# Row sums in a PSUM tile of their own, the first gathers moved ahead of a check, and fewer filler matmuls, in an attention and mixture-of-experts kernel

## The chip, the cores and the metric

The kernel runs on one core of one Trainium2 chip. The metric is the device time of one execution in microseconds (us), the median over several runs. Where the text gives a clock, it is the granted clock of TensorE: the share of full speed that the chip gave it, as a mean over the run or over the stretch named.

## The reference, cut to what matters

```python
# attention: 4 batches, 8 heads, 768 positions, head size 64; 8 global keys and a band of 96
scores = q @ k.T / 8 + bias;  a = softmax(scores where kept);  o = a @ v
x = o laid out as 3072 tokens x 512
# experts: 8, each takes exactly 384 tokens, chosen greedily by the sorted gate logits
logits = x @ w_gate
for (token, e) in sorted(logits, descending):
    if token is free and counts[e] < 384: assign it
out[tokens of e] = relu(x[tokens of e] @ w1[e]) @ w2[e]     # 512 -> 1024 -> 512
```

## The kernel before

Attention works on 16 pairs of heads. For the first six pairs the token rows are made at once: TensorE sums the weights of each row (`sums`), turns the output to token rows (`pn`), VectorE turns the sums (`dg`), takes the reciprocal (`rs`) and writes the scaled rows (`xb`). Sums and rows share one tile in PSUM, the buffer into which all these matmuls write. There are three such tiles in a ring (tag "ps"), and the scores of the next pair go through the same ring.

```python
        def token_matmuls(i, ot):
            ...
            pn = ps.tile([128, 8, 128], FP32, tag="ps", name=f"pn{i}")
            NS = S_ // 4
            sums = pn[:, 6:8, :].rearrange("p a x -> p (a x)")[:, 0:NS]
            ...                                   # 12 matmuls into sums
            if i < N_ATTN:
                token_transposes(pn, ot)          # 6 transposes into pn[:, 0:6]
            return pn, sums

        def gate_terms(i, sums):
            ...
            nc.vector.transpose(out=dg.rearrange("p c x -> p (c x)"), in_=sums)
            nc.vector.reciprocal(rs, dg[:, :, 0:2])
            ...
        def token_rows(i, pn, rs):                # xb = pn * rs
```

After the routing, the index of each expert's tokens is written (`idi`), then a flag that says whether the fast routing was valid (`fi`). GpSimd gathers the tokens by index, 128 rows at a time, three gathers for each expert. While the first ones are on the way, TensorE runs filler matmuls, meant to keep its clock up (with 2 of them, in fill2, the mean clock was 0.968 or 0.969 in all four runs; with 12, in fill12, 0.981 to 0.984 in all five).

```python
        nc.vector.tensor_single_scalar(out=idi, in_=pI, scalar=float(N_TOK // 2), op=ALU.add)
        if check is not None:
            ...
            nc.vector.tensor_single_scalar(out=fi, in_=fm, scalar=capf, op=ALU.is_gt)
    ...
        dispatch(tX, tR, tZ[:, 1, :])
        keep_busy(po[0], 14)
    ...
    gather(0)
    flag = nc.values_load(fi[0:1, 0:1], engines=mybir.ALL_ENGINES)
    ...
        with tc.manual_schedule(engines={ET.PE, ET.DVE, ET.Activation}):
            gather(1)
            to_columns(0)      # per gather: 4 transposes (px), copy to xT, then keep_busy(spare, 2)
            for e in range(N_EXP):
                layer1(e)                          # 32 matmuls into ph, ScalarE writes hT
                for _ in range(2):
                    next_weights(nc.vector)        # cast staged weights, start the next load
                if e + 2 < N_EXP:
                    gather(e + 2)
                if e + 1 < N_EXP:
                    to_columns(e + 1)              # 12 transposes (pxe)
                layer2(e)
                next_weights(nc.scalar)
```

The softmax here doesn't subtract the row's maximum and nothing guards it: scores larger than these inputs give would overflow.

## Time and profile before

| | before |
|---|---|
| time, median (range) | 283.92 us (283.36 to 284.98) |
| span of the profiled run | 284.8 us; that run itself took 286.62 us |
| TensorE busy | 261.7 us, 92% |

The profiled run is 2.7 us longer than the median of the timed ones. It has a stop of TensorE in the second expert.

The hand-over to the experts in the timeline of the kernel before. The columns are start (us), duration, engine, line, operation, written tile and read tiles, shapes, count, and in brackets the idle time before and what ended it. PE is TensorE, PEld its weight loads, DVE VectorE, ACT ScalarE, POOL GpSimd; "issue" means that nothing was seen to be waited for:

```profile
178.95 0.18 DVE L315 TENSOR_SCALAR idi<-bank 128x24 int32<-128x24 f32 x1 [0.38 <-PE bank L314]
179.60 0.14 DVE L319 TENSOR_SCALAR fi<-fm 1x1 int32<-1x1 f32 x1
180.02 1.26 POOL L873 DMA_INDIRECT xe<-x_tok,idi  x1 [42.03 <-DVE fi L319]
...
186.79 1.47 POOL L873 DMA_INDIRECT xe<-x_tok,idi  x1 [0.30 <-issue]
186.93 2.36 DVE L508 CAST w<-st 128x2048 bf16<-128x2048 f32 x2
```

The indices are there at 179.13 (178.95 + 0.18). The first gather starts 0.89 us later and is said to wait for fi. The line at 186.79 is the sixth gather, the last one for the second expert. The line under it is VectorE's two casts of weights.

### The profile page before, as it was taken

Reading aid. Unit: us, or ns where it says so; the run is one execution under the profiler, and the core shown is the slowest. Engines: PE = TensorE matmul, PEld = TensorE weight load, DVE = VectorE, ACT = ScalarE, POOL = GpSimd, SP = SyncE. Lnnn points to the kernel's source line nnn. Section 1 sums busy time; section 2 is a strip of 40 time slices with the busy share of each in tenths; the row PEclk is TensorE's granted clock in tenths of the full one; section 3 lists DMA queues with packets and bytes.
Section 4 is the critical chain, followed back from the end, with each engine's and each line's share of the span. In section 5 each row is a group of like instructions: output and inputs, shape, how many; then the busy total and the mean of one; then the engine's idle time right before and its main releaser. Section 6 shows DMA issues by size and latency. Waiting matters only on the chain. (4 is left out here: it accounts for less than half of the span.)

```text
span 284.8 us, 7265 instructions
## 1 busy us (share of the span) xinstructions
PE 261.7 (92%) x2890; PEld 178.2 (63%) x2890; DVE 182.5 (64%) x349; ACT 155.4 (55%) x256; POOL 128.9 (45%) x170
## 2 busy tenths in 40 slices
PE   7899999999999999999988885999699999999990
PEld 5777777777788787778756552355355556556550
DVE  3466978887788778887988889143444535635420
ACT  1888665575777777776125665043347347356330
POOL 8469425552455555533100000577675663513512
PEclk9999999999999999999999999599999999999998
DMA  7989997696759678220298777259899999996112
GB/s 175 267 193 224 261 274 213 170 319 214 210 146 247 200 241 244 77 77 3 87 396 296 204 275 254 64 184 378 265 349 400 387 387 377 383 333 270 74 59 88
DMA packets 58340, 65.98 MB, mean 232 GB/s; under 512 B 32960, under 2 KB 43712, under 8 KB 58304
## 3 DMA queue, kind: packets, MB, share of 16 engines
q1 hardware_dynamic: 53664, 55.67, 63.3%
q0 software_dynamic: 3072, 9.44, 8.6%
q10 hardware_dynamic: 1568, 0.39, 0.7%
q8 instruction: 23, 0.38, 0.6%
q14 instruction: 13, 0.11, 0.1%
HBM read 56.05 MB, written 9.44 MB: 230 GB/s over the span
## 5 line engine op out<-in xcount | busy, mean ns | idle before, releaser
L930 ACT ACTIVATE hT<-ph 128x384 bf16<-128x384 f32 x64 | 30.9, 490 | 52.1 <-PE ph L927 50.7
L873 POOL DMA_INDIRECT xe<-x_tok,idi x24 | 25.4, 1060 | 54.9 <-DVE fi L319 42.0
L619 ACT ACTIVATE P<-ps 128x860 f32<-128x860 f32 (+1 forms) x48 | 41.3, 892 | 14.4 <-PE ps L612 13.3
L612 PE MATMUL ps<-qT,kT 64*128 64x215 f32 (+2 forms) x448 | 44.1, 337 | 2.8 <-DVE qT L601 1.1
L927 PE MATMUL ph<-xT,w 128*128 128x384 bf16 x256 | 43.7, 326 | 3.1 <-issue 2.4
L945 POOL DMA_INDIRECT out_dram<-ot,idi x24 | 30.6, 1275 | 31.0 <-DVE ot L944 27.4
L942 PE MATMUL po<-w,hT 128*128 128x512 bf16 (+1 forms) x200 | 42.8, 370 | 0.0
L612 PEld LDWEIGHTS ps<-qT,kT 64*128 64x128 f32 x448 | 36.6, 187 | 8.8 <-PE ps L612 2.6
L627 DVE TENSOR_TENSOR P<-P,Wm 128x860 f32<-128x860 f32 (+1 forms) x32 | 32.6, 1055 | 11.7 <-ACT P L619 11.4
L669 PE MATMUL po<-P,vt 128*32 128x215 f32 (+4 forms) x1024 | 38.8, 302 | 0.0
L927 PEld LDWEIGHTS <-w 128*128 128x128 bf16 x256 | 25.0, 98 | 21.2 <-issue 4.3
L593 POOL COPY kT<-kT 128x56 f32<-128x56 f32 x16 | 11.6, 724 | 56.7 <-ACT kT L590 41.3
L669 PEld LDWEIGHTS po<-P,vt 128*32 128x32 f32 x1024 | 29.7, 110 | 9.7 <-issue 2.5
L944 DVE COPY ot<-po 128x512 f32<-128x512 f32 (+1 forms) x25 | 16.7, 670 | 28.5 <-PE po L942 20.2
L508 ACT CAST w<-st 128x1024 bf16<-128x1024 f32 (+1 forms) x23 | 33.4, 1451 | 0.0
L942 PEld LDWEIGHTS <-hT 128*128 128x128 bf16 x200 | 19.3, 98 | 20.4
L918 DVE COPY xT<-pxe 128x1536 bf16<-128x1536 bf16 x7 | 6.7, 958 | 22.4 <-PE pxe L917 22.4
L601 ACT COPY qT<-ptq 128x768 f32<-128x768 f32 x15 | 12.0, 802 | 16.2 <-PE ptq L580 16.2
L638 DVE TENSOR_TENSOR R<-P 128x950 f32<-128x950 f32 x16 | 18.9, 1180 | 0.0
L624 DVE TENSOR_TENSOR P<-P,Wm 128x860 f32<-128x860 f32 x16 | 16.9, 1055 | 2.0 <-DVE P L627 0.5
L508 DVE CAST w<-st 128x2048 bf16<-128x2048 f32 x15 | 18.0, 1239 | 0.0
L169 PE MATMUL po<-busy,c_ones_bf 128*128 128x512 bf16 x58 | 17.9, 433 | 0.0
(166 smaller groups left out, 362.9 us busy)
## 6 DMA issues: line engine op xcount, KB each, us to landing
st<-in_moe_w_dram SPq DMA_DIRECT2D x26, 1024.0 KB
st<-in_moe_w_dram SPq DMA_DIRECT2D x12, 512.0 KB
kr<-in_k_dram SPq DMA_DIRECT2D x15, 384.0 KB
qr<-in_q_dram SPq DMA_DIRECT2D x15, 384.0 KB
vt<-in_v_dram SPq DMA_DIRECT2D x32, 180.0 KB
x_tok<-xb SPq DMA_DIRECT2D x4, 768.0 KB
vt<-in_v_dram SPq DMA_DIRECT2D x32, 14.0 KB
qn<-in_q_dram ACTq DMA_DIRECT2D x2, 192.0 KB
```

The source lines that it names most:

```text
L169: nc.tensor.matmul(tile, lhsT=cs.ones_bf, rhs=cs.busy, start=True, stop=True)
L508: put(out=wt[n][:, a * half : a * half + a, :].rearrange("p a f -> p (a f)"), in_=st)
L612: nc.tensor.matmul(pt[:, t, off : off + widths[m]], lhsT=kk[64 * t : 64 * t + 64, m, :], rhs=qq[64 * t : 64 * t + 64, KT * m : KT * m + wi ...
L619: nc.scalar.activation(P, pt[:, :, 0:off], AF.Exp, scale=0.125)
L627: nc.vector.tensor_tensor(out=P, in0=P, in1=Wm[:, h0 : h0 + 2, w0 : w0 + off], op=ALU.mult)
L638: nc.vector.tensor_tensor(out=R[:, :, KT : 6 * KT].rearrange("p t (m q) -> p t m q", q=KT)[:, :, :, 0:tail], in0=P[:, :, QW : 6 * QW].rear ...
L669: nc.tensor.matmul(po[bank][64 * t + 32 * u : 64 * t + 32 * u + 32, c0 : c0 + n], lhsT=vv[:, t, m, 32 * u : 32 * u + 32], rhs=P[:, t, pc : ...
L873: nc.gpsimd.indirect_dma_start(out=xe_of[e][t], out_offset=None, in_=x_tok[:, :], in_offset=bass.IndirectOffsetOnAxis(ap=idi[:, TSLAB * e ...
L927: nc.tensor.matmul(ph, lhsT=w1_of(e)[:, kc, 128 * fc : 128 * fc + 128], rhs=xT_e[:, kc, :, :].rearrange("p t n -> p (t n)"), start=(kc == ...
L930: nc.scalar.activation(hT[:, fc, :], ph, AF.Relu)
L942: nc.tensor.matmul(po[:, 0:w], lhsT=hT[:, fc, 128 * t : 128 * t + 128], rhs=w2_of(e)[:, fc, c0 : c0 + w], start=(fc == 0), stop=(fc == NFC ...
L945: s = nc.gpsimd.indirect_dma_start(out=out[:, :], out_offset=bass.IndirectOffsetOnAxis(ap=idi[:, TSLAB * e + t : TSLAB * e + t + 1], axis= ...
```

## The change

The change has three parts. The row sums get a PSUM tile apart from the token rows (part A). The first expert's gathers go into the hand-made order, ahead of the count check (part B). The fillers go from 14 to 10, and from 2 to 1 between the transposes of the first expert (part C).

```diff
         nc.vector.tensor_single_scalar(out=idi, in_=pI, scalar=float(N_TOK // 2), op=ALU.add)
         if check is not None:
+            gather(0)
             nc.vector.tensor_reduce(out=fc8, ...)
 ...
-            pn = ps.tile([128, 8, 128], FP32, tag="ps", name=f"pn{i}")
+            pd = ps.tile([128, 2, 512], FP32, tag="ps", name=f"pd{i}")
             NS = S_ // 4
-            sums = pn[:, 6:8, :].rearrange("p a x -> p (a x)")[:, 0:NS]
+            sums = pd[:, 0, 0:NS]
 ...
-            if i < N_ATTN:
-                token_transposes(pn, ot)
-            return pn, sums
+            return sums
 ...
-                    pn, sums = token_matmuls(i - 2, oT[i - 2])
+                    sums = token_matmuls(i - 2, oT[i - 2])
                     rs = gate_terms(i - 2, sums)
                     if i - 2 < N_ATTN:
+                        pn = ps.tile([128, 8, 128], FP32, tag="ps", name=f"pn{i - 2}")
+                        token_transposes(pn, oT[i - 2])
                         token_rows(i - 2, pn, rs)
 ...
-        keep_busy(po[0], 14)
+        keep_busy(po[0], 10)
 ...                              # the definition of gather moves up, its call gather(0) goes from here
-    gather(0)
     flag = nc.values_load(fi[0:1, 0:1], engines=mybir.ALL_ENGINES)
 ...
-                        keep_busy(spare, 2)
+                        keep_busy(spare, 1)
```

More of the change, by code (lines that the diff above doesn't have):

```diff
@@ L817 @@
             add_tiles(NP - 1)
-            pn, sums = token_matmuls(NP - 2, oT[NP - 2])
+            sums = token_matmuls(NP - 2, oT[NP - 2])
             later.append((NP - 2, oT[NP - 2], gate_terms(NP - 2, sums)))
@@ L821 @@
             ot = attend(NP - 1)
-            pn, sums = token_matmuls(NP - 1, ot)
+            sums = token_matmuls(NP - 1, ot)
             later.append((NP - 1, ot, gate_terms(NP - 1, sums)))
@@ L846, in next_weights, with gather @@
                 fetched.append(fetch(stage, *late.pop(0)))
+    gp = ctx.enter_context(tc.tile_pool(name="gp", bufs=9))
+    xe_of = {}
+    def gather(e):
+        if e not in xe_of:
+            xe_of[e] = [gp.tile([128, DM], BF16, tag="xe", name=f"xe_{TSLAB * e + t}") for t in range(TSLAB)]
+        for t in range(TSLAB):
+            nc.gpsimd.indirect_dma_start(
+                out=xe_of[e][t], out_offset=None, in_=x_tok[:, :],
+                in_offset=bass.IndirectOffsetOnAxis(ap=idi[:, TSLAB * e + t : TSLAB * e + t + 1], axis=0),
+                bounds_check=N_TOK - 1, oob_is_err=False,
+            )
     with tc.manual_schedule(engines={ET.PE, ET.DVE, ET.Activation, ET.Pool}):
@@ L859 @@
         dispatch(tX, tR, tZ[:, 1, :])
-        keep_busy(po[0], 14)
+        keep_busy(po[0], 10)
     psx.close()
     kx.close()
-    gp = ctx.enter_context(tc.tile_pool(name="gp", bufs=9))
-    xe_of = {}
-    def gather(e):
-        if e not in xe_of:
-            xe_of[e] = [gp.tile([128, DM], BF16, tag="xe", name=f"xe_{TSLAB * e + t}") for t in range(TSLAB)]
-        for t in range(TSLAB):
-            nc.gpsimd.indirect_dma_start(
-                out=xe_of[e][t], out_offset=None, in_=x_tok[:, :],
-                in_offset=bass.IndirectOffsetOnAxis(ap=idi[:, TSLAB * e + t : TSLAB * e + t + 1], axis=0),
-                bounds_check=N_TOK - 1, oob_is_err=False,
-            )
-    gather(0)
     flag = nc.values_load(fi[0:1, 0:1], engines=mybir.ALL_ENGINES)
```

## The prediction

> **What bounds the kernel now.** I read the page's slices and its chain first, then the timeline stage by stage. The chain reaches back only to 184.66 us: it is the tail of the expert stage, where TensorE hardly stops. Before that lie attention (0 to 138 us), five routing rounds with the dispatch (138 to 179) and the hand-over to the first expert (179 to 187). So whatever is saved before 187 us should move the end by as much, if the stages in between keep their length. I looked for TensorE's stops in the two stages that the diff touches.
>
> Attention: the list of waits between 10 and 138 us (engine, line, what it waited for, total us, times, longest):
>
> ```profile
> DVE dg L709 <- PE pn L701: 7.9, 6, 1.7
> DVE dg L709 <- PE pn L691: 4.7, 7, 0.8
> PE ps L612 <- DVE xb L735: 0.8, 4, 0.3
> ```
>
> Six times VectorE's transpose of the row sums (dg) waits for the token transposes (L701), though it reads only what L691 wrote. TensorE in turn waits for the scaled copy xb before it may reuse the tile. TensorE's timeline (start, us, line, count), first a pair with token rows, then one without:
>
> ```profile
> 45.75 0.87 PE L701 MATMUL pn<-ident,oT 128*128 128x128 f32 x6
> 46.56 1.87 PE L612 MATMUL ps<-qT,kT 64*128 64x215 f32 x20
> 48.62 1.18 PE L612 MATMUL ps<-qT,kT 64*128 64x215 f32 x8 [0.19 <-DVE xb L735]
> ...
> 81.80 2.60 PE L612 MATMUL ps<-qT,kT 64*128 64x215 f32 x28
> 84.32 0.88 PE L580 MATMUL ptk<-ident,kn 128*128 128x128 f32 x6
> ```
>
> and VectorE beside the first of these:
>
> ```profile
> 46.66 0.38 DVE L709 STREAM_TRANSPOSE dg<-pn 128x192 f32<-128x192 f32 x1 [1.31 <-PE pn L701]
> ...
> 47.52 0.95 DVE L735 TENSOR_TENSOR xb<-pn,rs 128x768 bf16<-128x768 f32 x1
> ```
>
> The printed 0.19 us understates the stop. By starts, the 28 score matmuls take 2.52 us without token rows (81.80 to 84.32); with them 3.07, 2.98, 3.17, 2.99, 3.41 and 2.99 us in the six pairs.
>
> Hand-over:
>
> ```profile
> 178.73 5.83 PE L169 MATMUL po<-busy,c_ones_bf 128*128 128x512 bf16 x14
> 184.86 0.38 PE L907 MATMUL px<-c_ident_bf,xe 128*128 128x128 bf16 x4 [0.30 <-PEq L881]
> ...
> 186.16 0.39 PE L907 MATMUL px<-c_ident_bf,xe 128*128 128x128 bf16 x4
> 187.06 1.14 PE L927 MATMUL ph<-xT,w 128*128 128x384 bf16 x6 [0.51 <-issue]
> ```
>
> Fourteen filler matmuls fill the time until the gathered rows arrive; each takes 0.427 us, twice the 0.215 us between the fillers at 185.08. The windows' granted clock says why: 1.00 until 177.25, 0.50 until 184.0, then 1.00.
>
> [...]
>
> **The change part by part.**
>
> A, a tile of its own for the row sums (six pairs). No instruction is added or removed. In the built programs dg waits for the 12 row-sum matmuls instead of the 6 transposes behind them, and the transposes' wait is taken up by xb. At 46 us: the row sums end at 45.82 (45.31 + 0.51), so dg starts at about 45.86, not 46.66; VectorE had been idle since 45.36. xb keeps its 0.86 us behind dg: 46.72, just after the transposes' end at 46.62. It ends at 47.67, not 48.47. The next 8 score matmuls want to start at 48.15: 46.56 plus 1.59, which is 2.52 less the 0.93 us that 8 such matmuls take where nothing waits (30.89 to 31.82). Before, 48.62 was xb's end plus 0.15; now that would be 47.82, so the stop of 0.47 us goes. Over the pairs: 0.55, 0.46, 0.47, 0.47 and 0.47 us, **2.4 us**. The fifth pair (3.41) stops on an issue gap before xb matters, and 0.18 us of the third lies behind the wait; I leave both. The price is one more turn of three buffers. The pn tile now waits for ScalarE's copy of ptk, done some 3 us before (51.55 against 54.80 in the next pair); the scores behind it wait for the qT copy (45.60 against 46.5); the next wait for dg (46.24). None should bind. The later pairs, 7.59 us each, are TensorE back to back, so they only start earlier.
>
> B, the first gathers ahead of the count check. The page puts the gather's start at 180.02 on fi, which ends 0.61 us after idi, so the move seems worth 0.6 us. But the built programs are alike here: in both, GpSimd's gather waits for vector count 286, which idi raises; fi is 289. GpSimd's own order is the same too. **0 us.** The profile named the vector instruction that ended last before it.
>
> C, fewer fillers: 14 to 10, and 2 to 1 twice. Four fewer at 0.427 are 1.7 us: TensorE reaches the first transposes at about 183.15 instead of 184.86. There the data take over: the windows show the third gather's bytes between 184.5 and 185.5, so its transposes can't start before about 185.45, against 186.16. The first layer then starts near 186.35, not 187.06: **0.7 us**.
>
> Sum: 2.4 + 0 + 0.7 = 3.1 us off 283.9.
>
> **The rivals.** (1) The clock stays at half. Fillers now run 4.2 us instead of 5.9[...]. In the trace, the window from 177.3 to 180.7 had fillers for 57% of its length and did not bring the clock back[...]. If it fails, the first layer runs at half speed for some 3.4 to 6.8 us after 186.35, and costs half of that, 1.7 to 3.4 us, nearly all of the gain. I give this one chance in four for a given run. (2) A new wait in the buffer ring: the scores at 46.5 depend on VectorE (dg) where they depended on ScalarE. VectorE has 1.3 us of idle time ahead of each dg, which speaks against it; it would leave A near 1 us. (3) The saving is taken back later: the loads of the next pairs, or the weights. TensorE waits once for a load in attention (0.2 us), and no cast of weights waits in the expert stage; since all stages shift together I see no room for it. TensorE does stop for 1.9 us at 200.4 in the second expert, for a reason the trace doesn't name; if that follows the transfers and not TensorE, up to 0.7 us of C is lost. (4) B is real after all, and all three gathers start 0.6 us earlier: then C is worth 1.3 and the time is 280.2.
>
> **Range and chances.** 283.9 - 3.1 = 280.8; rival 1 at one in four with some 2.5 us adds 0.6, the issue gaps and (4) take away a little. I say **281.0 us**. Low end 279.6: A 3.1, C 1.3. High end 283.2: A halved, or the clock late in most runs. Two per cent faster is 278.2, 5.7 us less, more than all parts together at their best (A 3.5, B and C 1.3): chance 0.04. Slower by 2% needs a new wait in every pair: 0.02. Within 2%: 0.94.
>
> **What would show it.** A: dg starts right behind L691, its waits for L701 are gone, L612 no longer waits for xb, and the pair period falls from about 8.9 to 8.4 us; attention's end moves from 138 to about 135.6. B: the first gather still starts about 0.9 us after idi's end. C: the third px starts about 6.3 us after idi's end (7.0 before) and the clock is back to 1.00 before the first L927. I am wrong if L612 or L701 waits for DVE or ACT in the six pairs, if L927's first 32 matmuls take well over 5.5 us, or if the saving made by 138 us is no longer there at 180.

## The result, and the profile after

| | before | changed |
|---|---|---|
| time, median (range) of the same rounds | 283.84 us (283.36 to 284.98) | 280.99 us (280.20 to 281.95) |
| ratio of fast runs, 95% interval | | 0.9895 (0.9853 to 0.9938) |
| span of the profiled run | 284.8 us | 278.4 us (the fastest of its four runs) |

A ratio is the mean time of one kernel's fast runs over that of the other's in the same rounds, so it is not quite the ratio of the medians. The gain is 2.85 us by medians; 281.0 us was predicted. The total came out right, but two of its terms did not.

**Attention.** The list of waits of the changed kernel between 10 and 138 us (engine, tile, line, what it waited for, total us, times, longest) has one line of dg, and none of scores that wait for xb:

```profile
DVE dg L708 <- PE pd L692: 5.3, 10, 0.7
```

The changed kernel's timeline at the pair that the prediction shows (TensorE and VectorE together):

```profile
43.59 0.86 PE L692 MATMUL pd<-R,oneh 128*32 128x192 f32 x16
44.26 0.51 PE L692 MATMUL pd<-oT,Gw 128*32 128x192 f32 x8
44.70 0.87 PE L700 MATMUL pn<-ident,oT 128*128 128x128 f32 x6
44.84 0.38 DVE L708 STREAM_TRANSPOSE dg<-pd 128x192 f32<-128x192 f32 x1
45.50 2.60 PE L613 MATMUL ps<-qT,kT 64*128 64x215 f32 x28
45.88 0.94 DVE L734 TENSOR_TENSOR xb<-pn,rs 128x768 bf16<-128x768 f32 x1
48.03 0.87 PE L581 MATMUL ptk<-ident,kn 128*128 128x128 f32 x6
```

dg starts while the transposes run, 0.07 us after the modelled end of the sums. The scores run as one block: 48.03 minus 45.50 is 2.53 us, as in pairs without token rows. Starts of score blocks are now 8.40 us apart in these pairs. From the block ahead of the first of these pairs to the start of the last block attention takes 109.95 us (19.75 to 129.70); before, it took 113.40 (19.80 to 133.20). So 3.45 us went in this pair of profiles.

**Hand-over and first expert.** The changed kernel's timeline:

```profile
175.48 0.18 DVE L315 TENSOR_SCALAR idi<-bank 128x24 int32<-128x24 f32 x1 [0.38 <-PE bank L314]
...
176.55 1.26 POOL L857 DMA_INDIRECT xe<-x_tok,idi  x1 [42.05 <-DVE fi L320]
...
180.67 0.40 PE L907 MATMUL px<-c_ident_bf,xe 128*128 128x128 bf16 x4 [1.23 <-DMA xe<-x_tok,idi]
...
182.21 0.40 PE L907 MATMUL px<-c_ident_bf,xe 128*128 128x128 bf16 x4 [0.70 <-DMA xe<-x_tok,idi]
182.98 2.35 DVE L509 CAST w<-st 128x2048 bf16<-128x2048 f32 x2
183.12 5.36 PE L927 MATMUL ph<-xT,w 128*128 128x384 bf16 x32 [0.51 <-DVE xT L909]
183.34 2.12 POOL L857 DMA_INDIRECT xe<-x_tok,idi  x1 [0.30 <-issue]
...
189.60 0.40 PE L917 MATMUL pxe<-c_ident_bf,xe 128*128 128x128 bf16 x4 [0.67 <-DMA xe<-x_tok,idi]
```

The first gather is 0.89 us behind the indices (175.66 to 176.55), as before. The first layer starts at idi + 7.46 us (183.12 minus 175.66) against idi + 7.93 before, so C brought 0.47 us up to there, not 0.7: the third transposes wait for their rows until idi + 6.55, where I had said 6.3. Then something new appears. The sixth gather takes 2.12 us instead of 1.47, and the second expert's last transposes wait 0.67 us for its rows. On the page, the chain of work that ended last has an entry for DMA (2% of the span) that the one before lacks.

### The profile page after: what moved, and what is told of

The parts are those of the page before. It is cut to its first block, busy times and chain, and to the rows that moved or that the text cites.

```text
span 278.4 us, 7233 instructions
## 1 busy us (share of the span) xinstructions
PE 255.2 (92%) x2870; PEld 177.2 (64%) x2884; DVE 183.9 (66%) x349; ACT 155.1 (56%) x256; POOL 131.7 (47%) x170
## 5 line engine op out<-in xcount | busy, mean ns | idle before, releaser
L857 POOL DMA_INDIRECT xe<-x_tok,idi x24 | 26.7, 1111 | 51.7 <-DVE fi L320 42.1
L620 ACT ACTIVATE P<-ps 128x860 f32<-128x860 f32 (+1 forms) x48 | 40.7, 891 | 12.5 <-PE ps L613 11.7
L945 POOL DMA_INDIRECT out_dram<-ot,idi x24 | 29.7, 1238 | 31.0 <-DVE ot L944 27.4
L927 PE MATMUL ph<-xT,w 128*128 128x384 bf16 x256 | 42.9, 326 | 0.5 <-DVE xT L909 0.5
L613 PE MATMUL ps<-qT,kT 64*128 64x215 f32 (+2 forms) x448 | 42.1, 334 | 1.3 <-DVE qT L602 1.1
L594 POOL COPY kT<-kT 128x56 f32<-128x56 f32 x16 | 13.3, 832 | 49.0 <-ACT kT L591 37.6
L635 POOL COPY R<-P 128x240 f32<-128x240 f32 x16 | 15.7, 980 | 1.7 <-PE pd L692 1.4
```

The source lines that it names most:

```text
L613: nc.tensor.matmul(pt[:, t, off : off + widths[m]], lhsT=kk[64 * t : 64 * t + 64, m, :], rhs=qq[64 * t : 64 * t + 64, KT * m : KT * m + wi ...
L620: nc.scalar.activation(P, pt[:, :, 0:off], AF.Exp, scale=0.125)
L857: nc.gpsimd.indirect_dma_start(out=xe_of[e][t], out_offset=None, in_=x_tok[:, :], in_offset=bass.IndirectOffsetOnAxis(ap=idi[:, TSLAB * e ...
L927: nc.tensor.matmul(ph, lhsT=w1_of(e)[:, kc, 128 * fc : 128 * fc + 128], rhs=xT_e[:, kc, :, :].rearrange("p t n -> p (t n)"), start=(kc == ...
L945: s = nc.gpsimd.indirect_dma_start(out=out[:, :], out_offset=bass.IndirectOffsetOnAxis(ap=idi[:, TSLAB * e + t : TSLAB * e + t + 1], axis= ...
```

## The experiments

The first eight experiments ran on one chip, fill12, fill2 and fi_late on a second, hold2 on a third. Ratios are to the kernel before on the same chip. The kernel before took 283.8, 284.5 and 290.3 us on the three, so times of different chips are compared with care. All twelve gave correct results.

### Part A alone (a_only)

The kernel before with the lines of part A from the diff above, nothing else.

> The kernel before with part A alone (the row sums in a PSUM tile apart). My theory: A is nearly the whole gain, because the transpose of the sums (dg) no longer waits for the token transposes, so xb is written 0.8 us earlier and the 0.47 us stop per pair goes. Expected: all six score blocks at 2.52 us, the index write idi ends about 2.4 to 3.5 us earlier than in the kernel before (179.13), idi to first L927 unchanged at 7.9 us, time 2.4 to 3 us shorter, ratio 0.990. Rival: the parts need each other (a saving in attention is swallowed at the hand-over unless the fillers are cut too): then the ratio is 0.995 to 1.000.

Measured: 280.95 us against 283.79, ratio 0.9906 (0.9887 to 0.9925). The list of waits has again one line of dg:

```profile
DVE dg L707 <- PE pd L691: 5.4, 10, 0.7
```

A alone gives as much as the whole change. The rival, that the parts need each other, falls. Its first layer begins at idi + 7.99 us, and the first gather has not moved against idi.

### The transposes ahead of the sums (swap)

```diff
-                    sums = token_matmuls(i - 2, oT[i - 2])
-                    rs = gate_terms(i - 2, sums)
                     if i - 2 < N_ATTN:
                         pn = ps.tile([128, 8, 128], FP32, tag="ps", name=f"pn{i - 2}")
                         token_transposes(pn, oT[i - 2])
+                    sums = token_matmuls(i - 2, oT[i - 2])
+                    rs = gate_terms(i - 2, sums)
+                    if i - 2 < N_ATTN:
                         token_rows(i - 2, pn, rs)
```

> The changed kernel with the token transposes issued ahead of the row-sum matmuls, the two tiles still apart. It asks whether the tile apart is enough, or whether A's gain is that dg can start before the transposes have run. My theory: dg is bound by the end of both groups again (it comes behind the row sums, and these behind the transposes), starts about 0.8 us later after the start of the pair's block, and a stop of about 0.4 to 0.5 us per pair ahead of the next scores comes back: about 2.4 us slower than the changed kernel, ratio 0.997 to 0.999 against the kernel before, score blocks near 3.0 us. Rival: the tile apart alone is enough, since xb then has nothing to wait for but dg and the score tile is another buffer: score blocks stay at 2.52 us and the ratio is 0.989.

Measured: 282.30 us, ratio 0.9953 (0.9933 to 0.9973). Its timeline (VectorE, and PEld, TensorE's weight loads):

```profile
45.89 3.00 PE L613 MATMUL ps<-qT,kT 64*128 64x215 f32 x28
46.03 0.38 DVE L708 STREAM_TRANSPOSE dg<-pd 128x192 f32<-128x192 f32 x1 [1.12 <-PE pd L692]
...
46.89 0.95 DVE L734 TENSOR_TENSOR xb<-pn,rs 128x768 bf16<-128x768 f32 x1
...
47.89 0.67 PEld L613 LDWEIGHTS ps<-qT,kT 64*128 64x128 f32 x8 [0.46 <-DVE xb L734]
```

The tile is still apart, yet dg starts behind the scores' start again, and the scores' weight loads wait 0.46 us for xb. So it is the early start of dg that pays, not the tile as such. Whether sums placed elsewhere in the same tile would do as well, no run here asks. The loss is smaller than I expected: pairs are 8.64 us apart against 8.40, where a full stop of 0.47 would make 8.87, because in this order the block from the first q transpose to the first score is shorter (43.32 to 45.89, 2.57 us; in the changed kernel 42.78 to 45.50, 2.72). The stop of 0.40 us returns and 0.15 us is won elsewhere.

### Part B alone (b_only), and the check made late (fi_late)

b_only is the kernel before with the gather's lines of the diff. fi_late pushes fi away from idi:

```diff
             nc.vector.tensor_single_scalar(out=idi, ...)
         if check is not None:
+            for _ in range(4):
+                nc.vector.tensor_copy(out=mv, in_=OH)
             nc.vector.tensor_reduce(out=fc8, ...)
```

> The kernel before with part B alone (the first expert's gathers put into the hand-made order ahead of the count check). My theory: the built programs are alike at this place, GpSimd's gather waits for the vector instruction that writes idi in both, so nothing moves: first gather 0.89 us after idi's end, ratio 1.000. Rival: the profile's word holds that the gather waits for fi, 0.6 us behind idi: then the gather starts 0.3 us after idi and the kernel is 0.6 us faster (ratio 0.998).

> The kernel before with four copies on VectorE between the index write idi and the count check, so that fi is written at least 1.5 us later after idi. Theory: the gather waits for idi alone: it starts 0.9 us after idi's end as before, now well before fi, or at any rate not moved with it. Rival, the profile's word: the gather waits for fi and starts 0.3 us behind it, 2.4 us or more after idi. Time as before or, if the check itself comes to bind the first transposes, longer by up to 1 us.

Measured: b_only 283.33 us, ratio 0.9990 (0.9965 to 1.0015), its gather 0.89 us behind idi (178.43 to 179.32). fi_late 282.72 us in one run. The timeline of fi_late:

```profile
178.36 0.18 DVE L315 TENSOR_SCALAR idi<-bank 128x24 int32<-128x24 f32 x1 [0.38 <-PE bank L314]
178.46 1.33 DVE L318 COPY mv<-OH 128x576 f16<-128x576 f16 x4
179.42 1.26 POOL L875 DMA_INDIRECT xe<-x_tok,idi  x1 [42.02 <-DVE mv L318]
180.26 0.14 DVE L321 TENSOR_SCALAR fi<-fm 1x1 int32<-1x1 f32 x1
```

The gather starts at idi + 0.88 us, 0.84 us before fi is begun, and now the profile names a dummy copy as what released it. So it never waited for fi, and part B is worth nothing. The name in the brackets is whatever VectorE did last by then.

### Part C alone (c_only), the changed kernel again (again), and without C (ab)

c_only is the kernel before with 10 fillers and 1; ab is the changed kernel with 14 and 2; again is the changed kernel.

> The kernel before with part C alone (10 fillers instead of 14, 1 instead of 2 between the gathers' transposes). My theory: the data bind, not the fillers, as in the changed kernel: third group of transposes at idi + 6.5 us (7.03 before), first L927 at idi + 7.5 (7.93), 0.5 us faster, ratio 0.998. Rival: with fewer fillers the clock comes back only after L927 has begun, in some or all runs: 1.7 to 3.4 us slower in these, ratio 1.000 to 1.010.

> The changed kernel once more, beside the next three on one chip. Expected: ratio 0.989 to 0.991 against the kernel before.

> The changed kernel with part C undone (14 fillers and 2 again). New theory from the traces: C makes the first L927 start 0.5 us earlier, but this is given back: VectorE's casts of weights then start before the sixth gather and hold it until both have ended (2.12 us instead of 1.0), the weight loads that they release go ahead of its rows, and the second expert's third transposes wait 0.7 to 0.8 us; and in some runs the clock falls again in the first layer. So undoing C costs nothing: ratio equal to the changed kernel within 0.002, first L927 at idi + 7.9 to 8.1 us, first to second layer-one block 11.05 us (11.89 in the changed kernel), no wait of pxe on DMA. Rival, C as predicted: 0.5 to 0.7 us slower than the changed kernel, ratio higher by 0.002.

Measured: c_only 283.85 us, ratio 0.9996 (0.9976 to 1.0016). again 281.32, 0.9923 (0.9894 to 0.9952), just outside what was expected. ab 281.00, 0.9908 (0.9882 to 0.9934). No gain from C is seen, with or without A, though by time alone these intervals would not exclude one of 0.5 us. In the traces it is there at the first layer (idi + 7.49 us in c_only), and two things take it back, both first seen in these traces.

The first is a lower clock. TensorE's timeline of c_only has the first layer 1.5 us longer than the 5.36 us of the others:

```profile
186.98 6.85 PE L927 MATMUL ph<-xT,w 128*128 128x384 bf16 x32 [0.51 <-DVE xT L909]
```

The mean clock of c_only's six runs is 0.974 to 0.975 in three and 0.983 to 0.985 in the others. In the ten runs of the changed kernel (result and again) it is 0.969 to 0.977 in five, mean time 281.84 us, and 0.981 to 0.985 in five, mean time 280.82. In all 12 runs of the kernel before on that chip, and in all 18 of a_only, b_only and ab, it is 0.980 or more.

The second is the sixth gather. My expectation for ab failed: its first layer began at idi + 7.58 us, not 7.9 to 8.1, since the clock came back early in that run (idi + 4.3 us, against 5.0 in the kernel before) and the fillers ended sooner; and there too the casts came first and pxe waited 0.81 us. So it is not C as such, but when the casts start. In eight profiles ("casts" is the start of the two casts minus the start of the sixth gather; the last column runs from idi's end to the end of the span):

| kernel | casts | sixth gather | pxe waits | first to second layer-1 block | idi to end |
|---|---|---|---|---|---|
| a_only | +0.19 | 1.52 | no | 11.05 | 102.5 |
| b_only | +0.32 | 1.65 | no | 11.04 | 102.6 |
| fi_late | +0.12 | 1.45 | no | 11.05 | 102.4 |
| changed | -0.36 | 2.12 | 0.67 | 11.89 | 102.7 |
| again | -0.26 | 2.21 | 0.77 | 11.99 | 103.0 |
| ab | -0.22 | 2.25 | 0.81 | 12.03 | 103.1 |
| swap | -0.35 | 2.12 | 0.84 | 12.07 | 102.9 |
| c_only (clock low) | -0.32 | 2.15 | no | 12.55 | 103.4 |

In five of these eight the casts come first, and then the gather takes over 2.1 us; in all four of them with a full clock the next block is 0.8 to 1.0 us late. In c_only the slow first layer covers the wait. The kernel before is like a_only, b_only and fi_late: +0.14, 1.47, no wait. The timeline of a_only, where the gather is first, for comparison with that of the changed kernel:

```profile
183.99 1.52 POOL L873 DMA_INDIRECT xe<-x_tok,idi  x1 [0.31 <-issue]
184.18 2.36 DVE L508 CAST w<-st 128x2048 bf16<-128x2048 f32 x2
184.31 5.36 PE L927 MATMUL ph<-xT,w 128*128 128x384 bf16 x32 [0.52 <-DVE xT L909]
...
189.51 0.83 PE L917 MATMUL pxe<-c_ident_bf,xe 128*128 128x128 bf16 x12
```

In the changed kernel the gather ends at 185.46, 0.13 us after both casts (182.98 + 2.35 = 185.33); in a_only at 185.51, some 0.15 us after the first of them (184.18 + 1.18). In all eleven profiles in which it met a cast (the eight of the table, before, fill2 and fill12) the sixth gather ends 0.1 to 0.2 us after one of the two; the second to fourth gathers, which meet none, take 0.99 or 1.00 us. Starting first did not spare it: 0.06 to 0.32 us ahead of the casts (fill2, fi_late, before, a_only, b_only) it still took 1.40 to 1.65 us. What in the casts holds it, no trace shows.

A gather 0.6 us late would not by itself make pxe wait: it ends 3.5 us before those transposes could have begun (185.46 against 189.60 less the wait of 0.67). The transfers' view of the changed kernel, for 185.3 to 188.4 us, from about the gather's end (queue, kind, packets, MB, share of 16 engines):

```profile
q1 hardware_dynamic: 447, 0.92, 92.7%
```

and for 188.4 to 189.4 us:

```profile
q1 hardware_dynamic: 151, 0.28, 71.9%
q0 software_dynamic: 48, 0.13, 33.2%
```

The loads of weights (q1), issued as soon as a cast had freed its buffer (from 184.23, 0.03 us after the first cast's end and before the gather's; in a_only from 185.42, 0.09 us before the gather's), take 92.7% of the 16 engines' time; the 128 rows (0.13 MB on q0) come only behind 0.92 MB of them, from 188.4, some 3 us after the gather's end. In a_only the same 48 packets move between 186.2 and 187.3 us, ahead of nearly all of the load.

### The clock: two fillers (fill2) and twelve (fill12)

```diff
-        keep_busy(po[0], 10)
+        keep_busy(po[0], 2)        # fill2; fill12: 12, and keep_busy(spare, 1 + t) between transposes
```

> The changed kernel with 2 fillers instead of 10 ahead of the first transposes. Theory: TensorE is then idle for some 4 to 5 us more while it waits for the gathers; the data still bind (first transposes wait for DMA, third px at idi + 6.5, first L927 at idi + 7.5), but the clock is late in every run: mean granted clock 0.975 or less, the first layer's 32 matmuls take 6.5 to 8.5 us by starts instead of 5.2, and the time is 1 to 3 us above the changed kernel: 282 to 284, ratio 0.994 to 1.000. Rival, the clock follows something else than the fillers: mean clock spread as in the changed kernel (0.969 to 0.985) and ratio 0.990.

> The changed kernel with 12 fillers instead of 10 and 2 instead of 1 between the second and third transposes, without the dummy copies of hold12. It parts the two things that hold12 does. Theory: the fillers keep the clock (mean 0.98 or more in all runs, no slow first layer), but the casts still hold the sixth gather: 2.1 to 2.3 us, third pxe waits 0.7 to 0.8 us for DMA, first to second layer-one block 11.9 to 12.0 us. So some 0.8 us slower than hold12 (279.4): 280.2, ratio 0.988. Rival, all of hold12's gain is the clock: 279.4, ratio 0.985. Rival, all is the gather: as the changed kernel, ratio 0.990 to 0.992.

Measured: fill2 281.69 us, ratio 0.9906 (0.9876 to 0.9937), clock 0.968 or 0.969 in all four runs, first layer 7.08 us. The clock follows the fillers (in the ten runs with ten of them, result and again, it was 0.969 to 0.985). It cost less than I expected, because with the clock low (0.50 until 187.1) the first layer began later, at 183.54 (idi + 7.86); the casts then followed the gather (1.40 us) and nothing waited for rows. fill12: 280.32 us, ratio 0.9854 (0.9829 to 0.9880), clock 0.981 to 0.984 in all five runs, and the times within 0.3 us of each other; casts 0.33 us ahead, gather 2.14 us, pxe waits 0.78 us, next block after 12.00 us, all as expected. Its ratio was expected at 0.988; 0.9854 is nearer to that of its rival, that all of hold12's gain is the clock, so here the trace speaks for the theory and the ratio does not.

What cutting the fillers did is seen in the stretch that follows the clock's return. In every profile but that of fill2 (13.7 us) the half clock at the hand-over first lasts 6.8 us. In c_only and hold the full clock then lasts 3.4 us, and the half clock is back for another 3.4 (186.6 to 190.0 and 182.9 to 186.3). So I take TensorE's busy time in the 3.4 us after the full clock's return (stretch, length, busy time with count, clock, DMA share, GB/s), in the changed kernel:

```profile
179.00:182.40 3.40, 1.47 (x15) 0.99 0.30 84
```

in c_only, with the stretch behind it:

```profile
183.20:186.60 3.40, 1.48 (x14) 1.00 0.38 105
186.60:190.00 3.40, 3.02 (x10) 0.51 0.36 83
```

and in fill12:

```profile
181.00:184.40 3.40, 2.76 (x22) 1.00 0.36 111
```

With 1.47, 1.59 and 1.60 us (changed, again, swap) the clock stayed; with 1.48 and 1.40 (c_only, hold) it fell for the next 3.4 us. The edges of these stretches are known to some 0.1 us only: moving c_only's by 0.07 us turns its 1.48 into 1.41. So these five give no exact value at which it falls. With 2.2 to 2.8 us (fill12, hold12, hold2, ab, a_only, b_only, fi_late, before) it stayed in every profile. By cutting the fillers, C brought the busy time down to where both were seen; that the busy time decides is my reading of these profiles, not shown by a run of its own. The return of the full clock does not go by it alone: in fill2 2.37 us in 3.4 us did not bring it back (180.2 to 183.6) and 3.40 us did (183.6 to 187.0), but in the kernel before 3.40 us did not from 177.3 to 180.7 and did from 180.7 to 184.1. That the five slow runs of the changed kernel fell in the same way is an inference from their mean clock; they have no trace.

### The casts held back: hold, hold12, hold2

```diff
                 layer1(e)
+                if e == 0:
+                    idle = op.tile([128, DM], FP32, tag="ot", name="idle")
+                    for _ in range(3):                       # hold2: 2
+                        nc.vector.tensor_copy(out=idle, in_=spare)
                 for _ in range(2):
                     next_weights(nc.vector)
```

hold is the changed kernel with these lines. hold12 and hold2 have the fillers of fill12 too. The dummy copies read PSUM and their result is not used.

> The changed kernel with three dummy copies on VectorE (from PSUM, 0.69 us each) between the last copy of the first expert's columns and the first casts of weights, so that the casts start about 2.1 us later, behind the sixth gather. If the casts hold the gather: the sixth gather takes 1.0 us, the third pxe no longer waits for DMA, first to second layer-one block falls from 11.89 to 11.05, and the kernel is 0.8 us faster than the changed one in runs where the clock holds, although it does more work: ratio 0.986 to 0.988. Rival: the wait comes from the weight loads or the order of the queue alone: the sixth gather stays at 2.1 us or the wait stays, ratio as the changed kernel or higher.

> As hold, with 12 fillers instead of 10 and 2 instead of 1 between the second and third transposes, so that TensorE is idle less while it waits for the gathers. If the late clock comes from these idle stretches: the mean granted clock is 0.98 or more in all runs (0.969 to 0.983 in the changed kernel's), the first L927 still starts at idi + 7.5 us, and the times spread less than those of hold; ratio 0.986 to 0.987. Rival: the clock is as late as before, or the fillers push L927 to idi + 7.7 or more: ratio as hold or higher.

> As hold12 with two dummy copies instead of three: the casts then start about 1.4 us later than in fill12, at idi + 8.9 us, still behind the sixth gather (idi + 7.7 to 8.7). It asks for the gather's part of hold12's gain a second time, with another delay, since fill12's ratio to the kernel before (0.9854, taken on another chip) does not part from hold12's (0.985) although its time does (280.32 against 279.41 us). If what counts is only that the casts come after the sixth gather: sixth gather 1.0 us, no wait of the third pxe, first to second layer-one block 11.05 us, time 279.2 to 279.7 us. If the gain came from the clock alone: 280.3 us as fill12, or, if the shorter delay lets the casts hold the sixth gather in some runs, times between the two.

Measured: hold 281.32 us, ratio 0.9913 (0.9892 to 0.9934). Its gather takes 1.00 us and nothing waits for rows, as expected; but the clock was 0.974 to 0.980 in all six runs, the first layer took 6.61 us, and the gain was gone. Why the clock was low in all six, when the dummy copies start only as the first layer does, is not explained. The copies also put off the loads that the casts release (from 186.37 in hold12), so no run parts the held gather from the earlier loads: what is shown is that the two together cause the wait. hold12: 279.41 us, ratio 0.9850 (0.9829 to 0.9870), clock 0.981 to 0.985 in all five runs. Its timeline:

```profile
183.22 5.36 PE L927 MATMUL ph<-xT,w 128*128 128x384 bf16 x32 [0.52 <-DVE xT L909]
183.35 0.99 POOL L857 DMA_INDIRECT xe<-x_tok,idi  x1 [0.30 <-issue]
...
185.13 2.36 DVE L509 CAST w<-st 128x2048 bf16<-128x2048 f32 x2
...
188.41 0.83 PE L917 MATMUL pxe<-c_ident_bf,xe 128*128 128x128 bf16 x12
```

The first layer begins at idi + 7.54 us, the next block 11.04 us later (194.26), and idi to the end takes 102.0 us, against 102.5 in a_only: this is about the half microsecond that C was meant to bring. On one chip, hold12 is 1.9 us below the changed kernel and 1.5 us below a_only by medians. That is more than the 0.5 us of the stage and the late clock explain. Of the 1.1 us between the two profiled runs of a_only and hold12 (spans 278.8 and 277.7), 0.64 us lies ahead of idi's end (176.32 against 175.68), where neither fillers nor casts differ; in the eight profiles of the changed kernel and its variants other than swap, idi ends anywhere from 175.62 to 176.62. So part of it is scatter ahead of the hand-over.

hold2 ran on a chip where the kernel before took 290.32 us, with a clock of 0.970 in most of its runs, and hold2 284.40; the ratio of 0.9804 is not to be compared with the others. Its trace gives what was asked: casts 0.96 us behind the sixth gather, that gather 1.00 us, pxe without a wait. From its first to its second layer-one block it took 11.34 us, not 11.05, and the time expected, 279.2 to 279.7 us, was missed. In the second expert TensorE stopped twice, 1.11 and 1.37 us, on "issue", as in the profile of the kernel before; no run names that cause. How much of hold12's 0.9 us over fill12 is the gather stays open as a time: the two ran on different chips and their ratios agree within the interval. The traces show 0.96 us (12.00 against 11.04) at the place in question, and from idi's end to the end of the span 102.9 us in fill12 against 102.0 in hold12: one profile each.

## Why the prediction was right, point by point

- **The total** (281.0 us) was right: 280.99. It is right partly by luck, because two errors cancel: A came out some 0.4 us larger than said, and of C's 0.7 us nothing is seen.
- **A's mechanism** was right, in all its steps: dg behind the sums, xb earlier, no wait of the scores, 8.40 us for each pair, no new stop of TensorE in the ring. (The weight loads of the transposes are now said to wait 0.30 us for ScalarE's copy of qT, six times, which the prediction named as a sign of being wrong; before, the same 0.30 us stood under "issue", and the matmuls do not stop.) The trace, a_only and swap show it. **A's size** is the term that was too small (2.4 us): I counted five pairs and left the fifth one out, since there an issue gap stood in the profile. In the profile of b_only all six pairs stop alike, 0.46 us each, and from the first to the last score block it takes 112.71 us against 109.95 in the changed kernel: 2.76 us (2.45 against a_only, whose fifth pair has a gap of 0.31). a_only measured 2.84 us by medians, with an interval of 2.1 to 3.2, so by time alone 2.4 is not excluded.
- **B** is 0, as worked out from the built programs; fi_late shows that the profile's word was the wrong one.
- **C's** first step was nearly right (0.47 us at the first layer, not 0.7; the rows landed 0.2 us later than I read from the windows). The step that failed is that this start would carry through to the end: "no cast of weights waits in the expert stage; since all stages shift together I see no room for it", in rival 3. I had looked at whether the casts wait, not at who waits for the casts: GpSimd does (its sixth gather took 2.12 us instead of 1.47), and then the rows stand behind the loads that the casts release (pxe waits 0.67 us).
- **Rival 1**, the late clock, was real, and more frequent than one in four: five of ten runs of the changed kernel. It cost 1.0 us in time there, not 1.7 to 3.4, which was an estimate from 3.4 to 6.8 us of half clock in the first layer (3.0 us of it fell there in c_only's trace, 186.98 to 190.0); c_only's trace suggests why, since while the layer is slow the wait for rows is hidden.
- **Rival 4** (B worth 0.6 us) and **rival 2** (a wait in the ring) did not occur.

## What to carry to other kernels

When two results of one engine share a tile, the reader of the first can end up waiting for the writer of the second, as dg did here (1.31 us at the pair that the prediction shows); put the one that starts the longer chain apart and issue it first. A part that starts a stage earlier is worth something only if what the stage needs next also comes earlier: look at which other engine's instructions now start first, here VectorE's casts against GpSimd's gathers (the sixth took 2.12 us with the casts first, 1.00 us with them held behind it), and the loads that they release. And test a releaser that the profile names, by delaying it, before building on it; fillers that only wait went with the clock here (0.968 or 0.969 with two in fill2, 0.981 to 0.984 with twelve in fill12), so cut them with every run's clock in view, not one profile.
